# A one-core two-layer kernel: a new order from a planner that counts TensorE instructions in pieces of 256, and sums and denominators in one operation

## The chip, the core and the metric

The kernel runs on one core of one Trainium2 chip. The time is the device time of one launch in microseconds (us), the median of several runs. One further launch was taken by the profiler; the profile and the trace come from it. Engines are named as the profile names them: PE is TensorE (PEld its weight loads), DVE is VectorE, ACT is ScalarE, POOL is GpSimd, SP is SyncE, which issues most of the DMAs.

## The reference

Input `x` has 2048 rows of 512 values. Two blocks alternate, twice each, with the same weights:

```
x = x + A(layernorm(x));  x = x + B(layernorm(x))      # twice
A: q, k, v = x @ wqkv, 32 heads of 16
   phi(u) = [softmax(u @ w_phi), softmax(-u @ w_phi)]  # per head, 32 features
   kv = sum over rows of phi(k)^T v ;  z = sum over rows of phi(k)
   o  = (phi(q) @ kv) / (phi(q) . z + 1e-6) ;  return o @ wo
B: (relu(x @ W_gate) * (x @ W_up)) @ W_down            # 1376 hidden
```

The kernel does not form the softmax of the queries one by one. It keeps the exponentials (`expq`), and needs for each query and head two kinds of small numbers: the sum of the exponentials of each half (**feature sums**, made with the constant matrix `ZO`) and the product of the exponentials with `z` (parts of the **denominator**, made with `ZD`).

## The kernel before: its stages, and what sets its order

Everything stays in SBUF. The 16 tiles of 128 rows form five slabs of 2, 4, 4, 4 and 2 tiles. For each of two layers L and each slab st the stages are

- `layernorm` (L746 on): statistics on DVE, then the normalized tile (`ytile`, on ACT or DVE), then a transpose. The transpose is either a DMA (DMA_TRANSPOSE, L781), or full-size transposes on PE (L614), or, for a group of tiles, 16 transposes of 32 rows per tile (`strips`, L805).
- `keys` (L816 on): key and value products (four matmuls of 512 columns each per tile, `Wkp` and `wv`, issued by the helper `mm`, L610), exponentials of both signs on ACT (L833), their sums and reciprocals on DVE or ACT (L839 to L846), the value eviction, `vhat` on POOL or DVE (L853), and then the key-value sums: 32 matmuls per tile, each 34 columns wide (L865).
- `queries` (L913 on): query products (`Wqp`) and their exponentials (L923).
- `attend` (L926 on): 32 matmuls with `ZO` and 32 with `ZD` (both L938), an eviction of the first half (`Zs`, L951, ACT), a chain of five small operations (`zm`, `zden`, two activations, `aT`), the spreading of `aT` over the features (32 or 16 small matmuls with `EC` at L1034 for slabs 0 and 1, a round trip through DRAM for the others), the scaling of `expq`, 32 matmuls with `kvbd` (L986), four evictions (`oT`), and the product with `wo`.
- `glu`: gate and up products, ReLU (L1108), product (L1110), the down product with `Wd`, and the residual (L1056).

At the start, `load_x` and the weight loads fill SBUF (L632 to L665). `fold` (L712) multiplies the key and query weights by `w_phi` once. For the key weights it transposes 16 blocks on PE (L614), evicts them, and makes 16 matmuls against the block-diagonal matrix `BD` (L697); the query weights arrive transposed by DMA (L654).

The code only **records** operations. A list scheduler (`Program.schedule`) then places them: among the operations that are ready it takes the one that can start first, and among those the one with the lowest turn number. The turn numbers are one long list (`TURNS`, L140), one per operation. `ENG` says for single operations on which engine they run. The scheduler estimates for each operation an occupancy (`occ`) and a latency (`lat`), in ns, and `SWITCH` where PE changes between full-size and small-tile matmuls (`mode`). So an estimate changes no instruction, but it can change the order in which each engine's instructions stand. `plan` then works out the semaphore waits, and `emit` writes each engine's stream in that order; where an instruction has several waits, all but the last stand ahead of it as an instruction of their own.

The sums and the denominators are two operations unless `FUSEZ` names the slab; it is empty here:

```python
if together:
    op("pe", lambda e: (sums_q(e), dens(e))[1], reads=R_eq(st) + [R("ZO"), R("ZD"), R("ZD0")], writes=[zd], occ=2 * cost, lat=2 * cost + 200, name=f"zd{st}", mode=1)
else:
    op("pe", sums_q, reads=R_eq(st) + [R("ZO")], writes=[zd], occ=cost, lat=cost + 200, name=f"zz{st}", mode=1)
```

Of the kernel before, what the change touches and what calls it, by code (L numbers as in the profile page):

```python
# [6 lines left out]
FP32 = mybir.dt.float32  # L7
BF16 = mybir.dt.bfloat16
I32 = mybir.dt.int32
ALU = mybir.AluOpType  # L10
# [13 lines left out]
ENG = {'ap/a00/0': 'act',  # L24
 'ap/a02/3': 'dve',
 'ap/a11/0': 'act',
 'ap/a11/3': 'act',
 'ap/a12/0': 'act',
 'ap/a12/2': 'act',
 'ap/a12/3': 'act',  # L30
 'ap/a14/0': 'act',
 'ap/g00/0': 'act',
 'ap/g01/0': 'act',
 'ap/g01/2': 'act',
 'ap/g02/0': 'act',
 'ap/g03/1': 'act',
 'ap/g04/0': 'act',
 'ap/g11/1': 'act',
 'ap/g12/3': 'act',
 'ap/g13/1': 'act',  # L40
 'ap/g13/2': 'act',
# [3 lines left out]
 'em/10/00': 'act',  # L45
 'em/10/03': 'dve',
 'em/11/03': 'dve',
 'es/03/1': 'pool',
 'es/03/2': 'pool',
 'es/03/3': 'pool',  # L50
 'es/04/3': 'pool',
 'es/12/0': 'pool',
 'es/12/2': 'pool',
 'es/12/3': 'pool',
 'es/13/0': 'pool',
 'es/13/1': 'pool',
 'es/14/1': 'pool',
 'es/14/2': 'pool',
 'ot/01/2': 'dve',
 'ot/02/1': 'dve',  # L60
 'ot/02/3': 'dve',
 'ot/03/0': 'dve',
 'ot/03/1': 'dve',
 'ot/04/2': 'dve',
 'ot/11/1': 'dve',
 'ot/11/3': 'dve',
 'ot/12/1': 'dve',
 'ot/13/0': 'dve',
 'ot/13/1': 'dve',
 'ot/13/2': 'dve',  # L70
 'ot/14/2': 'dve',
 'rz/0/14': 'act',
 'rz/1/0': 'act',
 'rz/1/14': 'act',
 'rz/1/2': 'act',
 'rz/1/3': 'act',
 'rz/1/7': 'act',
 'rz/1/9': 'act',
 'vc/0/15': 'dve',
 'vc/0/5': 'dve',  # L80
 'vc/1/0': 'dve',
 'vc/1/1': 'dve',
 'vc/1/12': 'dve',
 'vc/1/13': 'dve',
 'vc/1/2': 'dve',
 'vc/1/4': 'dve',
 'vc/1/5': 'dve',
 'vh/0/1/0': 'dve',
 'vh/0/10/0': 'dve',
 'vh/0/11/1': 'dve',  # L90
 'vh/0/4/0': 'dve',
 'vh/0/5/1': 'dve',
 'vh/0/6/0': 'dve',
 'vh/1/0/0': 'dve',
 'vh/1/1/1': 'dve',
 'vh/1/11/0': 'dve',
 'vh/1/11/1': 'dve',
 'vh/1/12/0': 'dve',
 'vh/1/13/0': 'dve',
# [3 lines left out]
 'vh/1/3/1': 'dve',  # L103
 'vh/1/5/1': 'dve',
 'vh/1/7/0': 'dve',
 'vh/1/7/1': 'dve',
 'vh/1/8/1': 'dve',
 'xp/a02': 'pe',
 'xp/a14': 'sp',
 'xp/g11': 'sp',  # L110
 'yc/a02/00': 'act',
 'yc/a02/01': 'act',
 'yc/a04/1': 'dve',
 'yc/a10/02': 'dve',
 'yc/a12/00': 'dve',
 'yc/a13/00': 'dve',
 'yc/a13/02': 'dve',
 'yc/a13/03': 'act',
 'yc/a14/0': 'dve',
 'yc/a14/1': 'dve',  # L120
 'yc/g02/01': 'act',
 'yc/g02/02': 'dve',
 'yc/g03/02': 'dve',
 'yc/g03/03': 'act',
 'yc/g04/00': 'dve',
 'yc/g10/0': 'dve',
 'yc/g10/1': 'dve',
 'yc/g11/03': 'act',
 'yc/g12/02': 'dve',
 'yc/g12/03': 'act',  # L130
 'yc/g13/01': 'act',
 'yc/g13/02': 'dve'}
# [4 lines left out]
XQ = True  # L137
ZKPE = ()
FUSEZ = ()
TURNS = """  # L140
56 130 168 186 224 280 0 112 336 773 519 392 646 941 885 1404 1180 829 1068 1124 1348 1292 1236 1460 0 6 0 84 184 154 221 74 104 54 124 76 119 161 204
247 290 332 375 76 102 133 191 242 211 786 174 635 657 726 732 769 640 651 748 754 881 629 646 760 765 827 663 668 737 743 915 868 953 964 997 1199
873 942 975 992 1074 879 947 958 986 1266 885 936 970 981 1015 405 479 508 543 648 676 771 776 782 788 875 948 1134 1247 1362 1462 1526 1575 1580 1586
1631 1277 1321 1365 1409 1017 1039 1060 1082 1564 1516 1683 1849 1314 1914 2020 1743 1830 1851 1873 1959 1981 2003 2024 1929 1977 2078 2218 2211 2432
2284 2314 2529 3066 1343 1348 1354 1359 1420 1299 1304 1310 1315 1372 1387 1392 1398 1403 1468 1721 1727 1732 1738 2259 289 471 347 463 532 720 590
713 750 817 860 951 867 874 1061 992 1130 923 1223 1361 1428 1327 1395 1553 1591 1656 1699 1678 1895 1916 1938 1833 1785 1970 2390 2094 2601 2495 1504
1531 1613 1635 1483 1765 1787 1808 1689 1737 2282 2495 1881 2813 2707 2132 2154 2262 2283 2089 2111 2175 2219 2424 2472 2552 2728 2307 3328 2919 2046
2067 2240 2390 2718 2739 2761 2783 2520 2568 2770 2936 2978 3058 3216 3008 3439 3618 728 846 655 1006 1269 1559 1211 1494 1612 1679 2275 1949 1963
2355 2142 2025 2186 2561 2683 2731 2694 2660 2804 2826 2869 2891 2934 3063 3127 3214 3001 2943 3101 3279 3341 3414 3477 2847 2912 3171 3192 2955 2977
3084 3149 3389 3437 3510 3653 3602 3825 3719 3235 3257 3279 3300 3106 3343 3387 3515 3650 3485 3723 3849 3698 3931 4037 3322 3365 3408 3494 3537 3558  # L150
3623 3645 3794 3746 3891 4017 3842 4143 4249 4000 4399 4548 1567 2260 1501 2268 1625 1956 1791 2545 2616 2991 3209 3037 3051 3044 3272 3065 3134 3203
3412 3158 3285 3539 3818 3926 3947 3969 3839 3861 3882 3904 4019 4067 4140 4356 3954 4640 4421 3580 3602 3666 3688 3774 4130 4173 4216 4163 4115 4248
4398 4424 4527 4922 3710 3731 3753 3796 4054 4098 4238 4260 4211 4259 4440 4583 4472 4703 4809 4281 4453 4475 4496 4724 4745 4854 4951 4712 4664 4811
4985 5027 5197 5303 5047 5520 5597 1891 2537 2924 3049 3321 3533 3666 2878 3058 3890 3925 3999 4307 4400 4076 4152 4195 4324 4303 4346 4368 4518 4568
4616 4703 4904 4937 4760 4985 5091 4832 4897 4918 5016 4810 4973 4994 5123 5124 5172 5245 5371 5173 5542 5436 5371 5692 5747 5797 5841 5807 4648 4659
4669 4680 4691 4767 4778 4940 4979 5076 2641 2652 2663 2674 2685 2696 2707 4119 4376 4520 5219 5412 5885 5943 5977 6031 6063 6101 6167 6231 6316 6417
6291 6268 6350 6548 6691 6662 6613 6629 6746 6767 6789 6810 6832 6935 7015 6854 6875 6897 6918 6940 6993 7255 7177 7207 7245 7277 7334 7428 7433 7439
7444 7478 7184 7226 7303 7335 7416 7422 7472 7477 7526 2197 2346 2368 2498 2828 2635 4626 4875 5101 5166 5220 5316 4540 4561 4583 4702 4808 4856 2411
2433 2454 2476 2876 2780 5394 5469 5911 5990 6039 6079 6116 6159 6340 6570 6510 6451 6412 6696 6684 6749 6769 6868 6808 6817 6902 6971 7063 7111 7084
7159 7222 7450 7483 7504 7857 7157 7200 7287 7308 7368 7179 7244 7265 7330 7427 7136 7352 7373 7395 7487 7990 8068 7663 7822 7547 7814 7605 7829 8117  # L160
8152 8331 8233 8359 8240 8261 8200 8634 8380 8507 8253 7571 7579 7587 7595 8117 8169 8188 8197 8233 8338 8761 7604 7615 7713 7746 7757 7768 7778 7789
7724 7822 7877 7921 7931 7964 7986 8041 7829 8080 7888 7899 7910 7953 7975 7997 8008 8030 8325 8336 8391 8402 8413 8423 8434 8445 8069 8485 7636 7680
# [95 lines left out]
37644 37655 37666 37676 37687 37742 37760 37832 37338 37349 37414 37425 37786 37818 37829 37840 37360 37371 37393 37524 37611 37698 37731 37753 37879  # L258
37951 37447 37458 37469 37480 37491 37502 37513 37567 35994 36048 36081 36146 36254 36265 36809 37382 37607 37679 37589 37764 37796 37851 37949 37981
38036 38057 38079 38101 38122 38172 37872 37905 37927 37938 38025 38144 38155 38166 38177 38187 38209 38249 38303 37883 37894 37916 37970 38003 38014  # L260
38198 38220 38231 38242 38253 38292 38346 38253
"""

ENGINES = ("sp", "act", "pe", "dve", "pool")
# [961 lines left out]
```

## Time and profile before

| what | value |
|---|---|
| median of 3 runs | 393.76 us (393.55 to 395.07) |
| the profiled execution | 397.88 us, of it the span 396.3 us |
| granted PE clock over the span | 0.987 |
| PE busy | 382.0 us (96%), 4191 matmuls and as many weight loads |
| DVE, ACT, POOL busy | 274.3 us (69%), 196.3 us (50%), 68.5 us (17%) |
| first and last matmul | 1.55 us, 392.99 us |

The span is the time from the first to the last instruction of the profiled execution; 1.58 us lie around it. A matmul's end in the trace is modelled, so a busy PE may still be short of its best rate; the distance from one matmul's start to the next one's start is the safer number. On an undisturbed stretch this distance is 0.216 us for 512 columns and 0.109 us for 256.

### The profile page before, as it was taken

The page shows a single profiled execution, that of the slowest core. Times are in us where ns is not written, and L with a number is a line of the kernel's source. Part 1 is how long each engine was busy: PE and PEld are TensorE (multiplying, and loading weights), DVE is VectorE, ACT ScalarE, POOL GpSimd, SP SyncE. Part 2 cuts the span into 40 slices and gives each one's busy share as a digit, 9 for nine tenths or more (in the row PEclk, how much of TensorE's full clock was granted, in tenths as well). Part 3 has the DMA queues.
Part 4 walks back from the last instruction along what each step waited for, and adds up shares of the span by engine and source line. Part 5 has one row for each costly group of instructions (what it writes and reads, how often), then busy time and mean ns, then how long its engine had stood idle before and what let it go on. Part 6 is the DMA issues. An engine that isn't in the chain of part 4 may idle for free.

```text
span 396.3 us, 9884 instructions
## 1 busy us (share of the span) xinstructions
PE 382.0 (96%) x4191; PEld 203.0 (51%) x4191; DVE 274.3 (69%) x564; ACT 196.3 (50%) x427; POOL 68.5 (17%) x62
## 2 busy tenths in 40 slices
PE   5999999999999999999999979999999999999996
PEld 2544555584444544544565435558544444454564
DVE  7999967995856696775546978698684255753343
ACT  4999999860432254443425477883324121433111
POOL 0055880002500011510000523004331000000000
PEclk9799999999999999999999989999999999999999
DMA  8992200146320023010121120004552001121011
GB/s 259 324 273 56 30 3 3 45 116 120 75 60 2 12 29 80 1 17 2 40 48 23 30 31 2 4 12 129 114 145 42 13 15 41 41 54 54 2 41 46
DMA packets 51149, 24.09 MB, mean 61 GB/s; under 512 B 36801, under 2 KB 50081, under 8 KB 51105
## 3 DMA queue, kind: packets, MB, share of 16 engines
q1 hardware_dynamic: 50160, 23.11, 24.3%
q8 instruction: 33, 0.54, 0.6%
q10 hardware_dynamic: 944, 0.34, 0.3%
q14 instruction: 12, 0.09, 0.1%
HBM read 13.16 MB, written 2.42 MB: 39 GB/s over the span
## 4 chain that ended last, share of the span: by engine, by line
PE 58%; DVE 1%; issue 1%; DMA 1%; ACT 0%; SPq 0%
PE pb L610 54%; PE pb L865 1%; PE pb L938 1%; DMA yG<-ytile 1%; DVE expq L1052 1%; PE pb L986 1%; DVE x_sb L1126 0%; PE pb L1034 0%; DVE vsb L706 0%; DVE expq L1049 0%; ACT gate_sb L1108 0%; DVE hT L1110 0%; PE pb L614 0%; DVE zm L955 0%; DVE zden L957 0%
## 5 line engine op out<-in xcount | busy, mean ns | idle before, releaser
L1108 ACT ACTIVATE gate_sb<-pb 128x512 bf16<-128x512 f32 x80 | 47.1, 595 | 113.0 <-PE pb L610 95.2
L610 PE MATMUL pb<-Wd,hT 128*128 128x512 bf16 (+2 forms) x363 | 98.4, 373 | 0.0
L610 PE MATMUL pb<-yG,Wu 128*128 128x512 bf16 (+1 forms) x400 | 96.2, 336 | 0.9 <-DMA yG<-ytile 0.9
L610 PE MATMUL pb<-yG,Wg 128*128 128x512 bf16 (+1 forms) x400 | 96.2, 336 | 0.0
L1110 DVE TENSOR_TENSOR hT<-gate_sb,pb 128x512 bf16<-128x512 bf16 x80 | 53.6, 682 | 41.3 <-PE pb L610 34.2
L853 POOL TENSOR_TENSOR vhat<-vsb,rZk 128x544 bf16<-128x544 bf16 x44 | 47.4, 1101 | 151.7 <-DVE rZk L842 60.6
L1056 DVE TENSOR_TENSOR x_sb<-x_sb,pb 128x512 bf16<-128x512 bf16 x59 | 39.5, 681 | 38.3 <-PE pb L610 37.7
L610 PEld LDWEIGHTS pb<-yG,Wu 128*128 128x128 bf16 x400 | 39.0, 98 | 32.4 <-DMA yG<-ytile 1.4
L610 PEld LDWEIGHTS pb<-yG,Wg 128*128 128x128 bf16 x400 | 38.9, 98 | 30.5 <-issue 0.2
L610 PEld LDWEIGHTS pb<-Wd,hT 128*128 128x128 bf16 (+1 forms) x363 | 34.9, 98 | 34.8 <-DVE hT L1110 1.0
L839 DVE TENSOR_REDUCE Zk<-expk 128x64 f32<-128x1024 bf16 x32 | 38.3, 1204 | 7.1 <-ACT expk L833 6.8
L731 DVE BATCH_NORM_STATS2 stats<-x_sb 128x6 f32<-128x512 bf16 x60 | 40.2, 682 | 1.6 <-DMA x_sb<-in_A_x_dram 1.0
L610 PE MATMUL pb<-Wkp,yA 128*128 128x512 bf16 x128 | 40.5, 389 | 0.0
L610 PE MATMUL pb<-wv,yA 128*128 128x512 bf16 x128 | 40.1, 387 | 0.0
L833 ACT ACTIVATE expk<-pb 128x512 bf16<-128x512 f32 x64 | 35.2, 631 | 9.5 <-PE pb L610 8.2
L610 PE MATMUL pb<-wo_sb,oT 128*128 128x512 bf16 x128 | 37.7, 379 | 0.8 <-issue 0.5
L923 ACT ACTIVATE expq<-pb 128x512 bf16<-128x512 f32 x64 | 35.9, 642 | 2.9 <-PE pb L610 2.9
L610 PE MATMUL pb<-yA,Wqp 128*128 128x512 bf16 (+1 forms) x160 | 36.0, 344 | 0.4 <-ACT expk L833 0.3
L1019 POOL TENSOR_TENSOR expq<-expq,abT 128x1024 bf16<-128x1024 bf16 (+1 forms) x11 | 20.3, 1858 | 76.8 <-PE pb L610 61.8
L773 ACT ACTIVATE ytile<-x_sb,nmr,rstd 128x512 bf16<-128x512 bf16 x32 | 25.3, 829 | 5.7 <-DVE nmr L765 5.7
L1076 ACT ACTIVATE gate_sb<-pb 128x192 bf16<-128x192 f32 x16 | 5.3, 330 | 33.0 <-PE pb L610 32.5
L610 PEld LDWEIGHTS pb<-yA,Wqp 128*128 128x128 bf16 x160 | 14.8, 99 | 13.0 <-issue 1.3
(87 smaller groups left out, 341.5 us busy)
## 6 DMA issues: line engine op xcount, KB each, us to landing
abT<-spread SPq DMA_DIRECT2D x32, 128.0 KB
out_dram<-x_sb SPq DMA_DIRECT2D x15, 128.0 KB, 1.7
x_sb<-in_A_x_dram SPq DMA_DIRECT2D x3, 512.0 KB, 5.8
Wg<-in_B_W_gate_dram SPq DMA_DIRECT2D x1, 1280.0 KB, 6.8
Wu<-in_B_W_up_dram SPq DMA_DIRECT2D x1, 1280.0 KB, 11.5
Wd<-in_B_W_down_dram SPq DMA_DIRECT2D x1, 1280.0 KB, 13.3
abT<-spread SPq DMA_DIRECT2D x16, 64.0 KB
wv<-in_A_wqkv_dram SPq DMA_DIRECT2D x1, 512.0 KB
```

The source lines that it names most:

```text
L610: op("pe", lambda e: e.matmul(view(ps), lhsT, rhs, start=start, stop=stop), reads=reads, writes=[ps], occ=max(25.0, 0.4167 * n + 2.6), lat ...
L731: op("dve", lambda e: e.bn_stats(stats[:, t, :], src()), reads=[res], writes=[R("st", t)], occ=580, lat=680, name=f"bn{t}")
L773: op("act", (lambda t, yb: lambda e: e.activation(ytile[:, yb, :], x_sb[:, t, :], ACT.Identity, bias=nmr[:, t, :], scale=rstd[:, t, :]))(t ...
L833: op("act", (lambda i, s, pk: lambda e: e.activation(expk[:, i, s, :], full(pk), ACT.Exp, scale=1.0 - 2.0 * s))(i, s, pk), reads=[pk], wri ...
L839: op("dve", (lambda i, zb: lambda e: e.tensor_reduce(Zk[:, zb, :], expk[:, i, :, :].rearrange("p s (h f) -> p (s h) f", f=16), AX.X, ALU.a ...
L853: op(eng, (lambda i, s, vb, rz: lambda e: e.tensor_tensor(vhat[:, i, s, :, :], vsb[:, vb, :, :], rZk[:, rz, s * 32:(s + 1) * 32].unsqueeze ...
L923: op("act", (lambda c0, s, ps: lambda e: e.activation(eqv(st)[:, c0:c0 + per, s, :], ps.f32()[:, 0:per * n].rearrange("p (c n) -> p c n", ...
L1019: op(eng, lambda e: e.tensor_tensor(part, part, abT[:, c].rearrange("p (s n) -> p s n", s=2)[:, :, 0:n], ALU.mult), reads=Re + [R("abT", c ...
L1056: op("dve", lambda e: e.tensor_tensor(x_sb[:, t, :], x_sb[:, t, :], full(ps), ALU.add), reads=[R("x", t), ps], writes=[R("x", t)], occ=597 ...
L1076: op("act", (lambda gate, ps, half: lambda e: e.activation(gate, half(ps, 0), ACT.Relu))(gate, ps, half), reads=[ps], writes=[R("gate", gb ...
L1108: op("act", (lambda gb, pg, k: lambda e: e.activation(gate_sb[:, gb, 0:k], pg.f32()[:, 0:k], ACT.Relu))(gb, pg, k), reads=[pg], writes=[R( ...
L1110: op("dve", (lambda gb, hb, pu, k: lambda e: e.tensor_tensor(hT[:, hb, 0:k], gate_sb[:, gb, 0:k], pu.f32()[:, 0:k], ALU.mult))(gb, hb, pu, k),
```

## The change

All of the change is in the planner, in how it is fed, and in three places of the recorded work.

1. The scheduler counts PE's instructions, two for each matmul. At instruction 193, and every 256 after it, it puts a boundary, and keeps two boundaries at least 3.7 us apart (9 us in the first 25 us). Semaphore waits are not counted.
2. Estimates are changed: key-value sums, sums and denominators, the products at the former L986, and SP's DMA issue.
3. All turn numbers are new, and some 145 entries of `ENG` are added, taken out or changed.
4. `FUSEZ` names seven of the ten pairs of layer and slab: slabs 2 to 4 of the first layer and 1 to 4 of the second. There the 32 matmuls with `ZO` and the 32 with `ZD` follow each other as one operation.
5. The key weights come in four DMAs of 128 KB in place of two of 256 KB; `fold` transposes and evicts them by the row block that one DMA brings, in place of the column block that needs all four. `wv` is loaded through ACT's queue in place of SP's.
6. Layernorm "a10" transposes by DMA in place of `strips`.

A third way to make the sums (`ZALL`, with a DRAM tensor) is added in the code, but its list is empty, so it records nothing.

```diff
-FUSEZ = ()
+FUSEZ = ((0, 2), (0, 3), (0, 4), (1, 1), (1, 2), (1, 3), (1, 4))
+ZALL = ()
 TURNS = """
...
-    DMA_ISSUE = {"sp": 560.0, "act": 560.0, "pool": 1100.0}
+    DMA_ISSUE = {"sp": 600.0, "act": 560.0, "pool": 1100.0}
...
+    CHUNK, CHUNK0 = 256, 193
+    FETCH, FETCH0 = 3700.0, 9000.0
...
             if o.eng == "pe":
                 mode = o.mode
+                while chunk < count + 2 * o.ins:
+                    part = (chunk - count) / (2 * o.ins)
+                    at = s + o.occ * part
+                    came = crossed + (self.FETCH if at > 25000.0 else self.FETCH0) if chunk > self.CHUNK0 else 0.0
+                    if at < came:
+                        if chunk == count:
+                            s += came - at
+                        else:
+                            o.occ, o.lat = o.occ + came - at, o.lat + came - at
+                        at = came
+                    crossed = at
+                    chunk += self.CHUNK
+                count += 2 * o.ins
+            o.start = s
...
-        def load_wk(eng, c):
-            dma(eng, lambda e: e.dma_start(Wknat[:, c:c + 2, :], wqkv_v[:, c:c + 2, 512:1024]), writes=R_Wnat["k"][c:c + 2], nbytes=262144, name="ld wk")
+        def load_w(w, c, eng):
...
+                dma(ENG.get(f"ld/w{w}{c}", eng), lambda e: e.dma_start(Wnat[:, c:c + 1, :], wqkv_v[:, c:c + 1, o:o + 512]), writes=[R_Wnat[w][c]], nbytes=131072, name=f"ld w{w}{c}")
...
         def fold(w, Wnat, Wout):
-            for kc in range(0 if XQ and w == "q" else 4):
-                ps = bank(f"wt{w}{kc}")
-                for ic in range(4):
+            for ic in range(4):
+                if ic in XW[w]:
+                    continue
+                ps = bank(f"wt{w}{ic}")
+                for kc in range(4):
...
-                   writes=[ps], occ=225 * len(js), lat=200 + 225 * len(js), name=f"kv{st}", mode=1)
+                   writes=[ps], occ=286 * len(js) - 72, lat=128 + 286 * len(js), name=f"kv{st}", mode=1, ins=32 * len(js))
...
-            cost = 32 * max(8.0, w / 9.6)
+            cost = 41 + 3.33 * w
...
-               writes=pns, occ=80 + n, lat=280 + n, name=f"num{st}", mode=3)
+               writes=pns, occ=62 + 0.835 * n, lat=262 + 0.835 * n, name=f"num{st}", mode=3, ins=32)
```

## The prediction

> **What bounds the kernel now.** I read the page first, then the chain of waits, then PE's rows in order of time.
>
> ```profile
> PE 382.0 (96%) x4191; PEld 203.0 (51%) x4191; DVE 274.3 (69%) x564; ACT 196.3 (50%) x427; POOL 68.5 (17%) x62
> ...
> q8 instruction: 33, 0.54, 0.6%
> ```
>
> PE has work all the time, and no other engine comes near it. So time can only go where PE stands still or runs slowly. The second line is easily passed over: a queue that moves instructions, 33 transfers. PE's records in the trace are 4191 matmuls, 4191 weight loads and 80 of its sequencer (78 semaphore waits, 2 drains), 8462 in all, and 8462 / 33 = 256. PE's program is fetched in pieces of 256.
>
> ```profile
> 229.34 1.30 PE pb L865 x124
> 230.65 2.01 issue
> 232.66 0.20 PE pb L865 x4
> ```
>
> This is the chain of waits. "issue" means that PE waited for nothing the profile shows, in the middle of one operation. PE's own rows show four more such stops (their lengths in brackets in the rows): 0.32 us before 65.43, 0.49 before 172.84, 0.64 before 252.46 and 0.45 before 267.12. Counting all PE records, waits too, the five instructions at which PE goes on are numbers 2241, 4289, 5313, 6081 and 6849, each 193 plus a multiple of 256, to the instruction. From the passing of the boundary before to the resumption it is 3.76, 3.62, 4.5, 3.68 and 3.60 us. So PE stops where it uses up 256 instructions in less than some 3.65 us. A 512-column matmul pair takes 0.216 us, so 128 of them last 28 us and hide a fetch; small matmuls do not:
>
> ```profile
> 61.48 0.87 PE L938 MATMUL pb<-expq,ZD 128*32 128x64 bf16 x64
> 62.17 0.63 PE L938 MATMUL pb<-expq,ZO 128*32 128x128 bf16 x32
> 62.73 1.70 PE L610 MATMUL pb<-yA,Wqp 128*128 128x256 bf16 x11
> ```
>
> Start to start, 64 pairs (128 instructions) pass in 0.69 us. The five stops cost, start to start and less the usual distance, 0.55 + 0.62 + 2.34 + 0.87 + 0.61 = 5.0 us.
>
> ```profile
> 235.60 1.06 PE L610 MATMUL pb<-Wkp,yA 128*128 128x512 bf16 x2
> ...
> 239.45 0.81 PE L610 MATMUL pb<-Wkp,yA 128*128 128x512 bf16 x3
> ```
>
> After the longest stop, from 233.89 to 237.29, eight 512-column matmuls stand 0.427 us apart, not 0.216: the granted clock was halved for 3.4 us. Price 8 x 0.21 = 1.7 us. All other waits of PE after 28 us add up to some 2.1 us (1.04 at 92.6 for a transpose DMA, 0.38 at 157.1, the rest under 0.3 each).
>
> ```profile
> 7.69 0.62 PE L614 MATMUL pb<-ident,hT 128*128 128x128 bf16 x8 [2.02 <-DMA hT<-in_A_wqkv_dram]
> ...
> 12.30 1.91 PE L610 MATMUL pb<-wv,yA 128*128 128x512 bf16 x4
> ```
>
> At the start PE waits for the second half of the key weights until 7.69, then for `BD` until 10.28, and dense work begins at 12.30, at half clock until 15.4.
>
> **The change, part by part.** The profiled execution took 397.88 us, its span 396.3; the median of the plain runs is 393.76, that is 4.1 less. I work out differences and put them on the median; what the plain runs lack of the stops above cannot be seen.
>
> *Small-tile changes of PE.* Counted over both instruction orders, PE changes between full-size and small-tile forms 87 times before and 73 times after: seven fused pairs, and the layernorm that no longer uses strips. A change costs some 0.1 us: 32 `ZO` matmuls with full-size work behind them take 0.56 us (62.17 to 62.73), and in the rows where another small group of the same form follows 0.447. 14 x 0.1 = 1.4 us, plus the 32 strip transposes, 0.2: **-1.6 us**. Both ends: 14 x 0.08 (entering a small group) and 14 x 0.115 (leaving one), -1.3 to -1.8. What fusing delays (`Zs` can only be evicted after both halves, and sums can't be taken before the key-value sums are there) lies 0.45 us earlier in a chain through ACT and DVE that other matmuls cover; uncovered it costs 0.45 us in each of seven slabs, 3.2 at worst, which I keep for the range.
>
> *The pieces.* The planner now holds boundaries 3.7 us apart, but it counts two for each matmul and no waits. The trace counts the waits, so the real boundaries come earlier in the order than the planner's, by some 30 instructions at 65 us and 80 at the end. I added up the rows' distances over the new order, between real boundaries (193 + 256k, waits counted). By the planner's own count no piece is under 3.6 us. By the real count four are:
> - 1985 to 2241: the end of a 64-column `ZD` group, three 128-column groups (3 x 0.447), two changes, three 512-column matmuls (0.65), 26 of `EC` (0.2): 2.4 us, 1.25 short.
> - 4545 to 4801: four and one of 256 columns, three of 512, 119 of L865 (1.0): 2.3 us, 1.35 short.
> - 5569 to 5825: 60 of L865, five of 512, 32 of L865, 31 of `ZO`: 2.2 us, 1.45 short.
> - 6337 to 6593: 11 of `ZO`, three groups of 0.447, 20 of the 512-column `kvbd`: 1.9 us, 1.75 short.
>
> The same sum over the order of before gives 0.43, 0.72, 1.65, 0.93 and 0.69, near the five stops, and a sixth, 1.09 before 5825, that did not come: the boundary ahead of it lay in dense 512-column work, and there the fetch began 1.5 us before PE reached it. The 4545 boundary lies in 256-column work, so its stop may be hidden too. New stops 4.5 to 5.8 against 5.0: **+0.2 us**, from -0.6 (and less, where a data wait fills the same gap) to +1.0.
>
> [...]
>
> *The clock.* Only a stop of over 2 us halved it in the row of before; the new ones are at most 1.75. In the profiled execution that is -1.7 us, in the plain runs, which may not have had it, 0. I take **-0.5**.
>
> *The start.* SP's queue has 1024 KB of `x` ahead of the two key-weight DMAs in place of 896, and `wv` (512 KB) now moves beside them from ACT's queue. At 324 GB/s (second slice of the page) that is 0.4 us later, up to 2.0 with equal shares: last landing 8.1 to 9.7 in place of 7.69. But `BD` now stands in DVE's order right behind the first statistics, so that from the landing it is transposes 0.4, eviction 0.75, products 0.4 to 0.8: dense work begins at 9.7 to 11.7 in place of 12.30. Until 15.4 the clock is half, so half of the gain stays: **-0.5 us**, from -1.3 to +1.0 (the three evictions of `Wkp` stand in a row on ACT).
>
> *All else.* New turn numbers move every instruction by a little. Counts by engine hardly change (ACT loses six half-size `oT` evictions to DVE, six reciprocals go from DVE to ACT as two activations of 0.27 us each); DVE stays near 69%. SP issues two layernorm transposes more. The 2.1 us of data waits can become 1 to 5; I take them as unchanged.
>
> Sum: -1.6 + 0.2 - 0.5 - 0.5 = -2.4 us, so 393.76 - 2.4 = **391.4 us**; in a profiled execution some 395.5.
>
> **Rivals.**
> *Stops gone.* If PE's real boundaries are where the planner puts them (no waits counted), all stops go: -1.6 - 5.0 - 0.5 - 0.5 = -7.6, 386.2 us. Against it: with waits left out, the sum over the order of before gives no stop at 232.66 and a false one of 2.2 us.
> *Clock, slower.* The four stops of 1.25 to 1.75 us each halve the clock for the next 3.4 us; each then costs 1.7 more. All four: -1.6 + 1.0 - 0.5 + 6.8 = +5.7, 399.5; three (-1.6 + 0.2 - 0.5 + 5.1 = +3.2) 397.0; two 395.3. It decides from the third such halving on. For it: the halving came after 2.2 us idle, a part of its 3.4 us. Against it: stops of 0.6 to 0.9 did nothing. [...]
> *New data waits.* The two or three us saved come back as waits (a late DRAM round trip of `aT`, a late transpose, the fused sums' 0.45 us a slab): +1.5 to +5 on 391.4, 393 to 396.5.
>
> **How the numbers follow.** 0.5% of 393.76 is 2.0 us, about what a measurement of this kernel tells from no change; faster means under 391.8, slower over 395.7. Forecast 0.62 (own range 389 to 394; 0.38 of it faster, 0.24 within 0.5%), stops gone 0.08 (faster), data waits 0.18 (0.13 within, 0.05 slower), clock 0.12 (slower). That is 0.46, 0.37 and 0.17. The range 387.0 to 396.5 takes in the forecast and the data waits and leaves out most of the other two.
>
> **What would show it.** In the changed profile: "issue" stops of PE at records 193 + 256k, the longest ahead of 6593, 5825 and 2241, and none over 2 us; some 73 changes; no halved clock after the first 16 us; `wv` matmuls before 12 us. The forecast is wrong if PE shows stops at other places, no stops, or more than 4 us of waits for ACT, DVE or DMAs after 28 us.

## The result, and the profile after

The changed kernel takes 396.32 us (median of 18 runs, 394.64 to 398.63) against 394.17 us for the kernel before (median of 18, 393.06 to 396.42). The ratio is 1.0048, with a 95% interval of 1.0028 to 1.0069: slower by some 2 us, where 2.4 us less was forecast. A second set of runs side by side gave 1.0026 (0.9992 to 1.006). The loss is small, but the sign of the forecast was wrong.

The page of the changed kernel, in the two lines that answer to those of before (busy time of each engine; the instruction queue):

```profile
PE 373.6 (95%) x4107; PEld 203.3 (52%) x4159; DVE 274.2 (69%) x561; ACT 195.8 (50%) x431; POOL 71.2 (18%) x63
...
q8 instruction: 32, 0.52, 0.6%
```

PE is busy for 8 us less than in the profile of before (382.0), in a span that is only 1.6 us shorter (394.7 against 396.3). A part of that is not real: this trace holds 4107 matmuls for 4159 weight loads, so 52 records of matmuls are missing, where the trace of before has all of its 4191. Up to the last matmul PE is idle for 17.6 us, of which 2.7 lie at missing records; before it was 11.0. So it stands still some 4 us more. Its rows in order of time show where (start, length, form, count; in brackets the idle time before the row and what ended it):

```profile
62.96 0.38 PE L1143 MATMUL pb<-aT,EC 32*128 32x64 bf16 x26
64.73 0.23 PE L1143 MATMUL pb<-aT,EC 32*128 32x64 bf16 x6 [1.39 <-issue]
...
68.19 0.40 PE L1143 MATMUL pb<-aT,EC 32*128 32x128 bf16 x16 [0.58 <-DVE expq L1161]
...
70.52 0.23 PE L1022 MATMUL pb<-expq,ZD 128*32 128x128 bf16 x4
71.36 0.57 PE L1022 MATMUL pb<-expq,ZD 128*32 128x128 bf16 x28 [0.61 <-issue]
...
244.69 0.45 PE L1022 MATMUL pb<-expq,ZO 128*32 128x64 bf16 x31
246.21 0.19 PE L1022 MATMUL pb<-expq,ZO 128*32 128x64 bf16 x1 [1.06 <-issue]
...
259.19 0.61 PE L1095 MATMUL pb<-expq,kvbd 32*32 32x512 bf16 x20
260.74 0.43 PE L1095 MATMUL pb<-expq,kvbd 32*32 32x512 bf16 x12 [0.94 <-issue]
```

Read the counts first: 26 and 6, 4 and 28, 31 and 1, 20 and 12. Each pair is one operation cut in two with no wait named, at instructions 2241, 2497, 5825 and 6593, all 193 plus a multiple of 256. Three of them are those that the prediction named as the longest. From start to start, less the usual distance, they cost some 5.2 us together, inside the 4.5 to 5.8 forecast. The 0.58 us before 68.19 is of another kind: PE waits for DVE.

To see where an execution loses time I add up the rows' usual distances over the instruction order (372.94 us before, 371.48 after, so the new order is 1.46 us shorter) and look at how far PE is behind that sum. This is what each stretch adds, in us, for the profiled executions. The stretches are counted in the sum of rows, which runs some 10 us behind the clock of the trace:

| execution | its time | first 50 us | 50 to 75 | 75 to 220 | 220 to 255 | behind 255 |
|---|---|---|---|---|---|---|
| before (that of the prediction) | 397.88 | 10.40 | 1.33 | 6.00 | 1.96 | -0.12 |
| before, `b_same` | 391.98 | 10.07 | 1.33 | 1.48 | 0.84 | -0.07 |
| before, `b_again` | 396.72 | 10.12 | 1.32 | 5.64 | 1.47 | -0.13 |
| after | 396.52 | 9.63 | 3.61 | 2.42 | 3.67 | -0.14 |
| after, `a_again` | 394.53 | 8.76 | 3.64 | 1.57 | 3.36 | -0.15 |

Two things stand out. The new order loses 2.3 us more in the attention of the first layer (50 to 75) and about 2 us more in that of the second (220 to 255), alike in both executions. And the old order loses some 6 us between 75 and 220 in two executions of three, and 1.5 in the third.

### The profile page after: what moved, and what is told of

It reads as the page before. It is cut to its first block, busy times and chain, and to the rows that moved or that the text cites. A ratio compares the mean times of both kernels' runs of the same rounds, so it can differ in the third digit from the quotient of the medians.

```text
span 394.7 us, 9764 instructions
## 1 busy us (share of the span) xinstructions
PE 373.6 (95%) x4107; PEld 203.3 (52%) x4159; DVE 274.2 (69%) x561; ACT 195.8 (50%) x431; POOL 71.2 (18%) x63
## 3 DMA queue, kind: packets, MB, share of 16 engines
HBM read 13.16 MB, written 2.42 MB: 39 GB/s over the span
## 4 chain that ended last, share of the span: by engine, by line
PE 73%; ACT 12%; DVE 6%; DMA 5%; issue 2%; SPq 1%; DVEq 0%
PE pb L679 68%; ACT expk L906 4%; ACT expq L1007 3%; DMA hT<-in_A_wqkv_dram 2%; PE pb L1022 2%; ACT ytile L846 2%; PE pb L938 1%; DMA yG<-ytile 1%; DVE expq L1161 1%; PE pb L1095 1%; DMA abT<-spread 1%; ACT vsb L780 1%; DVE Zk L912 1%; ACT gate_sb L1217 1%; DMA yA<-ytile 1%
## 5 line engine op out<-in xcount | busy, mean ns | idle before, releaser
L679 PE MATMUL pb<-Wd,hT 128*128 128x512 bf16 (+3 forms) x353 | 93.8, 372 | 0.7 <-issue 0.5
L679 PE MATMUL pb<-yG,Wu 128*128 128x512 bf16 (+1 forms) x394 | 92.9, 336 | 1.0 <-DMA yG<-ytile 0.3
L679 PE MATMUL pb<-yG,Wg 128*128 128x512 bf16 (+1 forms) x394 | 91.7, 336 | 0.4 <-issue 0.2
L679 PE MATMUL pb<-wv,yA 128*128 128x512 bf16 x119 | 37.3, 379 | 1.3 <-DMA yA<-ytile 0.5
L679 PE MATMUL pb<-Wkp,yA 128*128 128x512 bf16 x122 | 37.9, 379 | 0.6 <-issue 0.3
L1128 POOL TENSOR_TENSOR expq<-expq,abT 128x1024 bf16<-128x1024 bf16 (+1 forms) x13 | 23.6, 1824 | 79.6 <-PE pb L679 53.2
L679 PE MATMUL pb<-wo_sb,oT 128*128 128x512 bf16 x123 | 34.9, 379 | 0.7 <-issue 0.3
L679 PE MATMUL pb<-yA,Wqp 128*128 128x512 bf16 (+1 forms) x150 | 32.3, 334 | 1.8 <-issue 1.0
## 6 DMA issues: line engine op xcount, KB each, us to landing
Wd<-in_B_W_down_dram SPq DMA_DIRECT2D x1, 1280.0 KB, 15.4
```

What stands on the lines that cost most here:

```text
L679: op("pe", lambda e: e.matmul(view(ps), lhsT, rhs, start=start, stop=stop), reads=reads, writes=[ps], occ=max(25.0, 0.4167 * n + 2.6), lat ...
L1128: op(eng, lambda e: e.tensor_tensor(part, part, abT[:, c].rearrange("p (s n) -> p s n", s=2)[:, :, 0:n], ALU.mult), reads=Re + [R("abT", c ...
```

## The experiments

My theory was that the place of the 256-instruction boundaries among the small tiles decides, and that the forecast had compared with an unusual execution. The rival was that the new order (its fused operations, or the rest of it) makes new waits for data.

### The same kernels again

No edit. `b_same` and `b_again` are the kernel before, `a_again` is the changed one.

> The kernel before again, unchanged, for a second profile of it with its granted clock. Theory 1 (the profiled execution of before that the prediction was built on was a slow one, by its halved clock and by some more): span near 392.5 us, device time 394 +-1, the five stops at the same instructions (2241, 4289, 5313, 6081, 6849), no halved clock in the middle in most runs. Rival (the halved clock behind the 2.2 us stop belongs to every run): span near 396 again, with eight 512-column matmuls 0.43 us apart behind 232.7.

> The kernel before a third time, for its stops: 5.0 us and a halved clock in the execution that the prediction read (397.88 us), 1.3 us and none in b_same's (391.98). If 5.0 was the usual amount: stops of 4 to 5.5 us behind 28 us, a halved clock behind 16 us, a profiled time near 397. If it was an outlier and the stops differ from execution to execution: 1 to 3.5 us, 392 to 395.

> The changed kernel a second time. If its stops are as little fixed as those of before: 2 to 6 us, at other boundaries than 2241, 5825 and 6593. If they are fixed by the order (the boundaries lie among small tiles that follow waits, where the sequencer cannot be ahead): stops at these three again, 4 to 5.5 us, 395.5 to 397.

`b_same`: 394.27 us, ratio to before 0.9989 (0.996 to 1.0019). `b_again`: 394.38, ratio 0.9989 (0.9956 to 1.0022). `a_again`: 395.86, ratio 1.0026 (0.9992 to 1.006).

PE's rows at the key-value sums, first in `b_again`, then in `b_same`:

```profile
228.88 1.38 PE L865 MATMUL pb<-vhat,expk 128*32 128x34 bf16 x124
232.00 0.20 PE L865 MATMUL pb<-vhat,expk 128*32 128x34 bf16 x4 [1.74 <-issue]
...
233.78 1.06 PE L610 MATMUL pb<-Wkp,yA 128*128 128x512 bf16 x2
```

```profile
228.26 1.43 PE L865 MATMUL pb<-vhat,expk 128*32 128x34 bf16 x128
...
232.01 0.81 PE L610 MATMUL pb<-yA,Wqp 128*128 128x512 bf16 x3
```

It is the same program. In `b_again` the operation is cut at 124 and 4 and stands for 1.74 us, and the 512-column matmuls behind it are 0.43 us apart (two take 1.06, and 0.59 at the full clock): the stop and the halved clock that the prediction had read. In `b_same` all 128 run in one row, and three 512-column matmuls take 0.81, the full rate. What differs is the transfer of the instruction queue (q8) that belongs to the boundary before, 5057 (193 + 19 x 256): it began 2.9 us before PE came to that boundary in `b_same`, and 1.6 to 1.7 us after it in the two others. All stops of before behind 28 us, start to start and less the usual distance, are 5.0, 1.3 and 4.1 us in the three executions; those of after are 5.2 and 5.0, at the same four boundaries both times. So the stops of the old order come and go, and those of the new one stood at the same places in both of its traces. The execution that the forecast was read from had the most of them, and was 3.7 us above its own median. But `b_again` is near it, as the first half of its expectation said, so a long stop at 5313 is no rarity. The plain runs say more: the six sets of runs of before beside these experiments hold 143 executions with a median of 394.2 us. Only 5 took longer than 397.88, and only 1 less than the 391.98 of `b_same`. The traces of before lie near the two ends.

### Moving the boundaries

Tiny matmuls at the end of the warm-up, where PE waits for the input anyway (3.09 us ahead of 8.21 in the changed kernel's trace), move every later boundary to an earlier place in an unchanged order:

```diff
+        def warm_up(e, i):
+            ins = e.matmul(full(warm), ones[:, 0:128], ones[:, 0:512], start=True, stop=True)
+            for k in range(SHIFT if i == NWARM - 1 else 0):
+                q = 32 * (k % 4)
+                ins = e.matmul(warm.f32()[q:q + 32, 0:34], ones[:, 0:32], ones[:, 0:34], start=True, stop=True, skip_group_check=True, tile_position=(0, q))
+            return ins
```

> The changed kernel; the last warm-up operation issues 102 more tiny matmuls (34 columns) whose results nobody reads, so that all piece boundaries lie 204 instructions earlier in the same order. Theory of the pieces (a stop where 256 PE instructions, waits counted, pass in under 3.65 us): the sum of the short pieces falls from 5.8 (measured stops 4.4) to 2.3 us, almost all of it near the L0 attention; the time falls by 2 to 3.4 us against the changed kernel, to about 393.5, if the extra matmuls lie in PE's wait for the first transposed tile (3.1 us). Rival (stops come from waiting data or from where the planner put its boundaries): no change, or up to 2 us slower for the extra matmuls.

> The changed kernel with 40 more tiny matmuls at the end of the warm-up (results unread): boundaries 80 instructions earlier, the worst place found for this order. Theory of the pieces: short pieces sum to 9.3 in place of 5.8 us, stops ahead of records 1985 (1.6), 5313 (1.9), 5825 (1.0), 6081 (0.7) and 6593 (1.9), so +2 to +3.5 us against the changed kernel, about 399. Rival (data waits set the end): no change within 1 us.

> The kernel before with 50 more tiny matmuls at the end of the warm-up (results unread): boundaries 100 instructions earlier. Theory of the pieces: short pieces fall from 5.5 to 2.1 us, the stops ahead of 4289, 5313 and 6849 are gone, so -2 to -3.4 us against the kernel before, about 391.5. Rival: no change.

> Before with 124 tiny matmuls at the end of its warm-up, the boundaries 248 instructions earlier, at nearly the worst place for this order: short pieces 6.3 us by the program (2.1 in b_shift50, 5.5 in before), of it 3.2 between 62 and 220 and 2.7 behind 220. If the order of before suffers from the boundaries as that of after does (a_shift40 against a_shift102: 7.9 us measured for 7.0 by the program): 396.5 to 398. If the old order is proof against them, since its small tiles stand apart and the sequencer runs ahead: 393 to 394.5.

| kernel | median us | ratio to before (95%) | short pieces by the rows |
|---|---|---|---|
| `a_shift102` | 394.35 | 0.9986 (0.9954 to 1.0018) | 2.3 |
| `a_shift40` | 402.25 | 1.0194 (1.0152 to 1.0236) | 9.3 |
| `b_shift50` | 393.09 | 0.9961 (0.9933 to 0.999) | 2.1 |
| `b_shift124` | 395.6 | 1.0033 (1.0002 to 1.0065) | 6.3 |

With nothing else changed, the place of the boundaries moves the new order by 0.0208, that is 8 us, and the old one by 0.0072, 2.8 us. PE's rows of `a_shift40`:

```profile
28.41 0.62 PE L947 MATMUL pb<-vhat,expk 128*32 128x34 bf16 x59
32.75 0.22 PE L947 MATMUL pb<-vhat,expk 128*32 128x34 bf16 x5 [3.72 <-issue]
...
35.44 1.06 PE L679 MATMUL pb<-Wkp,yA 128*128 128x512 bf16 x2
```

One stop of 3.72 us, at a time when the weights' DMAs still run in the changed kernel's trace (165 GB/s from 28 to 32 us, 5 from 32 to 36), and half clock behind it (512-column matmuls 0.42 to 0.43 us apart). This one place makes 6 of the 9.3 us between the profiled executions of `a_shift40` (403.89) and `a_shift102` (394.59), and the expectation had no stop there. Set against the changed kernel itself (1.0048 and 1.0026), `a_shift102` (0.9986) is 1.6 to 2.4 us faster: moving the boundaries alone takes back what the changed kernel had lost (its interval lies clear of the first set's, and overlaps that of the second). So the boundaries are shown to matter. `b_shift50`, the old order with 50 tiny matmuls, has the lowest ratio of this study, and its interval lies below 1. The sizes were not well foretold: `a_shift102` and `b_shift50` came out 0.9 and 1.6 us above their expectations, `a_shift40` 3 us above, and `b_shift124` between its two.

But the pair `a_shift102` and `b_shift50` also speaks for the rival. Their short pieces are the same (2.3 and 2.1), and the new order, 1.46 us shorter by its rows, is still 0.0025, 1.0 us, slower, though the two intervals overlap. By these numbers some 2.4 us go to something else.

### The stop by itself

`b_tail` puts 1536 independent small matmuls of three widths behind the last instruction of PE:

```diff
+            for width, times in ((34, 512), (64, 512), (128, 512)):
+                for k in range(times):
+                    q = 32 * (k % 4)
+                    ins = e.matmul(tail.f32()[q:q + 32, 0:width], ones[:, 0:32], ones[:, 0:width], start=True, stop=True, skip_group_check=True, tile_position=(0, q))
```

> Before with a ladder of 1536 independent small matmuls on TensorE behind its last one (its outputs go unused): 512 of 34 columns, 512 of 64, 512 of 128, all 32x32 tiles on four row quarters' columns in turn. It measures the disputed cost by itself: 256 instructions are 128 matmuls, by the rows 2.1, 3.5 and 7.1 us. If a piece that passes in under 3.65 us makes TensorE stop: 3.65 us for each piece of the first two widths, 7.1 for the third, 57 us in all, 450 to 453. If the instructions come in time whatever the pace: 8.4 + 14 + 28 = 51 us, 444 to 446, and no gaps in the ladder.

432.24 us in one execution, 38 us more than before, where 51 or 57 were expected: both expectations were wrong on the work, because these matmuls, on four column groups in turn, pass faster than I had worked out (128 of 34 columns in 1.2 us, not 2.1). The rows settle the question all the same:

```profile
388.04 2.02 PE L1176 MATMUL pb<-yG 128*32 128x34 bf16 x218
392.21 1.19 PE L1176 MATMUL pb<-yG 128*32 128x34 bf16 x128 [2.16 <-issue]
395.66 1.23 PE L1176 MATMUL pb<-yG 128*32 128x34 bf16 x128 [2.26 <-issue]
399.39 1.70 PE L1176 MATMUL pb<-yG 128*32 128x34 bf16 x128 [2.50 <-issue]
```

128 matmuls with their weight loads are 256 instructions. They run in 1.2 us (1.7 in the last row, at half clock), then PE stands for 2.2 to 2.5 us with nothing to wait for. From 392.21 on, ten pieces take 3.70 us in the mean from start to start (3.45 to 4.0), at all three widths. So this ladder shows the cost of a boundary bare, among small tiles. Among large ones it doesn't show: in the trace of before the last 313 matmuls, of 192 to 512 columns, make 626 instructions with their weight loads and hold three boundaries (343.4, 367.9 and 387.5 us); they run for 54.06 us without a stop, no two starts over 0.22 us apart:

```profile
338.50 54.06 PE pb L610 x313
```

### Fusing in the planner's hands

`a_unfused102` and `a_unfused12` are the changed kernel with `FUSEZ` empty and seven turns added; `b_fused58` and `b_fused82` the kernel before with the `FUSEZ` of after and seven turns left out. The numbers are those of the tiny matmuls. The cut is from the second pair; the first has it the other way round.

```diff
-FUSEZ = ()
+FUSEZ = ((0, 2), (0, 3), (0, 4), (1, 1), (1, 2), (1, 3), (1, 4))
```

> The turn numbers, engines and loads of after with nothing fused (seven turns added for the denominators, one product behind the sums), and 102 tiny matmuls: short pieces 2.3 us, as in a_shift102, its partner, which took 394.35, and at the same places (all among the small tiles of the first layer's attention). Changes of tile size rise from 73 to 84, the sum of rows by 1.1. Theory: 395.4 (394.6 to 396.2). Rival 'fusing itself costs': 394.3 or less.

> As a_unfused102 with 12 tiny matmuls: short pieces 1.6 us, of which 0.1 among the first layer's small tiles (2.3 in a_unfused102) and 1.4 among those of the second. If a stop costs its length wherever it falls: 0.7 less than a_unfused102, 394.7 by the theory. If a stop in the first layer's attention costs more than its length there, since DVE and ACT run out of work behind it and PE then waits for them in turn, up to twice: 392.5 to 393.8.

> The order of before with the seven fused operations alone (the turns of the seven denominator operations are left out), and 58 tiny matmuls more at the end of the warm-up, so that the boundaries lie where the pieces that are too short sum to 2.2 us by the program (2.1 in b_shift50, its partner, which took 393.09). Changes of tile size fall from 87 to 80. Theory 'a change of tile costs its 0.19 us, and the pieces their shortness': 393.1 - 0.7 = 392.4 (391.6 to 393.2). Rival 'fusing itself costs': the feature sums come out one product later, and ACT and DVE, which wait for them, start later: 393.6 or more.

> As b_fused58, with 82 tiny matmuls: short pieces 1.7 us by the program, 0.4 to 0.5 of them among the small tiles of the first layer's attention (1.05 in b_fused58). Theory: 391.9 (391.0 to 392.8), the fastest so far. Rival 'fusing itself costs': 393.2 or more.

| kernel | median us | ratio to before (95%) |
|---|---|---|
| `a_unfused102` | 394.57 | 0.9993 (0.9966 to 1.002) |
| `a_unfused12` | 396.0 | 1.0049 (1.002 to 1.0079) |
| `b_fused58` | 394.54 | 0.9999 (0.9974 to 1.0024) |
| `b_fused82` | 396.52 | 1.0043 (1.0019 to 1.0068) |

Taking the fused operations out of the new order adds 1.1 us to the sum of rows and 0.3 us to the time, within the intervals. Putting them into the old one takes 0.7 off the sum and adds 1.5 us against `b_shift50`, with intervals that overlap too. By these numbers the saved changes of tile size are given back. `a_unfused12` and `b_fused82` missed their forecasts by 1.3 and 4.6 us, and the sum of short pieces alone doesn't explain them. In their traces PE waits for data, which the sum leaves out: 1.4 us near 159 for a layernorm transpose and 0.8 near 258 for ACT in `b_fused82`, 1.0 near 282 for a transpose in `a_unfused12`. These kernels also don't part cause from cause: the planner, with other estimates, moved other matmuls as well (in `b_fused58` eight query matmuls that had stood between the numerators and the spread now stand ahead of the numerators).

### Fusing with nothing else moved

To part them, the order of before was written out for every engine and kept, with 50 tiny matmuls as in `b_shift50`, and only the denominators' 32 products of six slabs were put right behind the sums:

```diff
+        for line in ORDER.values():
+            line = [self.ops[int(k)] for k in line.split()]
+            for a, b in zip(line, line[1:]):
+                b.odeps.add(a.idx)
```

`b_fix50` does that. `b_two50` gives the denominators a PSUM bank of their own, so that ACT may copy the sums while PE goes on. `b_bank50` is `b_fix50` with every bank where before has it. `b_port50` also keeps which DVE operation each GpSimd multiply waits for. `b_first50` is `b_port50` with only the first layer's slabs fused. (With no slab fused this last form should be the program of `b_shift50`; that was not run.) `a_two102` does to the new order what `b_two50` does to the old one.

> The order of before on every engine written out and kept, with six fused operations (slabs 2 to 4 of both layers) where the sums stood, and the 50 tiny matmuls of b_shift50, its partner (393.09): so nothing moves but the denominators' 32 products. Sum of rows 0.5 less than b_shift50's, short pieces 0.6 more (2.8 to 2.1). Theory 'changes of tile and short pieces are all': 393.2 (392.6 to 393.8). Rival 'the sums come late': ACT copies them only when the fused operation has ended, 0.2 to 0.6 us later for each slab, and the chain behind (DVE, ACT, spread matmuls) is late by it six times: 394 to 395.

> As b_fix50, instruction for instruction on TensorE, but sums and denominators are two operations with a PSUM bank each, so ACT may copy the sums while TensorE makes the denominators. Theory: as b_fix50. Rival 'the sums come late': it gives back what b_fix50 lost, 392.6 to 393.3.

> The order of after on every engine written out and kept, with 102 tiny matmuls as in a_shift102, its partner (394.35), but sums and denominators of the seven fused slabs as two operations with a PSUM bank each, so the sums may be copied 0.2 to 0.6 us earlier; short pieces as in the partner (2.3). If the late sums are what the new order loses to the old one: 393.0 to 393.8. If not: 394.3 (393.9 to 394.8).

> b_fix50 again, but with every PSUM bank where before has it: b_fix50 had kept the order and let the planner choose the banks anew, and TensorE then waited for banks that ScalarE's evictions released late (1.7 us between 262 and 290 us alone). Now the instructions of TensorE, VectorE and ScalarE stand as in b_shift50 (393.09), its partner, except that the denominators' 32 products of six slabs stand right behind the sums. Sum of rows 0.5 less, short pieces 0.6 more (2.8 to 2.1). If banks were what b_fix50 lost, and fusing itself costs nothing: 393.2 (392.6 to 393.8). If the late sums cost: 394 to 395, with waits for DVE and ACT at the spread matmuls behind each fused slab.

> b_bank50 again (398.69), but GpSimd's multiplies wait for the same VectorE operations as in before. In b_bank50 the planner, whose times had moved, let two of them go ahead of VectorE's, and the trace shows VectorE's aT product taking 1.96 us for 0.41 and its expq product 2.61 for 0.69, each while a GpSimd multiply of 2.1 us ran: 3.5 us in all. Now order, banks and this order of the two engines are those of b_shift50 (393.09), and only the denominators' products of six slabs have moved. If those two meetings were the loss: 395.2 (394.6 to 395.8). If fusing by itself costs nothing beyond rows and short pieces: 393.2. If the loss is elsewhere: 398 or more.

> As b_port50, with only the three slabs of the first layer fused. Sum of rows 0.2 less than b_shift50's (393.09), short pieces 0.6 more, of them 0.6 where the first fused operation now stands (53 us of the rows). If fusing costs through short pieces alone: 393.5. If the sums' late copy costs as well, 0.4 us or so at the spread matmuls (TensorE waited 0.9 us for ScalarE there in b_bank50): 393.9 to 394.4. The difference to b_port50 is what the second layer's three slabs cost.

| kernel | median us | ratio to before (95%) | against its partner |
|---|---|---|---|
| `b_fix50` | 398.56 | 1.0134 (1.0105 to 1.0162) | +6.8 us |
| `b_two50` | 397.98 | 1.0112 (1.0081 to 1.0143) | +6.0 us |
| `b_bank50` | 398.69 | 1.01 (1.0054 to 1.0146) | +5.5 us |
| `b_port50` | 395.43 | 1.0024 (1.0005 to 1.0044) | +2.5 us |
| `b_first50` | 394.4 | 0.9987 (0.9959 to 1.0015) | +1.0 us |
| `a_two102` | 394.79 | 1.0003 (0.9978 to 1.0029) | +0.7 us |

The last column is the difference of the ratios times 394 us, the partner being `b_shift50` or, in the last row, `a_shift102`.

The banks were not it: `b_bank50` loses as much as `b_fix50`, against my theory of the moment. What the first three share is seen on DVE, here in `b_bank50` (start, length), and on POOL:

```profile
268.36 1.96 DVE L1110 TENSOR_TENSOR aT<-Zs,zr 128x256 bf16<-128x256 f32 x1
...
273.71 2.61 DVE L1169 TENSOR_TENSOR expq<-expq,abT 128x1024 bf16<-128x1024 bf16 x1
```

```profile
267.91 2.13 POOL L1169 TENSOR_TENSOR expq<-expq,abT 128x1024 bf16<-128x1024 bf16 x1 [24.10 <-PE pb L751]
271.52 4.26 POOL L1169 TENSOR_TENSOR expq<-expq,abT 128x1024 bf16<-128x1024 bf16 x2 [1.48 <-DVE x_sb L1206]
```

The same two operations take 0.41 and 0.68 us in `b_shift50`. In `b_fix50` they take 1.88 and 2.61, in `b_two50` 1.68 and 2.60. In `b_bank50` each ends 0.3 to 0.5 us after a GpSimd multiply that began before it: 1.55 + 1.93 = 3.5 us more on DVE. With the fused operations' times the planner had let POOL go first. `b_port50` puts this back and is 3.3 us faster than `b_bank50` by the medians, 3.0 by the ratios, near the 395.2 that was expected. In both products the loss is near what was left of the GpSimd multiply when the product began: 1.68 us for the first and, with the two multiplies of the second row taken as equally long, 2.07 for the second.

What `b_port50` still loses is 2.5 us, where the rows promised a gain of 0.5 and the short pieces a loss of 0.6. Not all that its trace shows is the price of fusing. That execution was the slowest of its twelve (397.14), and has this ahead of the first fused operation:

```profile
30.13 0.25 PE L964 MATMUL pb<-ident,ytile 32*128 32x32 bf16 x13 [1.75 <-issue]
...
31.09 1.84 PE L760 MATMUL pb<-wv,yA 128*128 128x512 bf16 x4
```

It is a stop of 1.75 us with half clock behind it, where `b_shift50` stops for 1.03 us at the same instruction and goes on at full clock; 1.9 us of the distance between the two traces arise here. `b_first50`, the same up to this point, has 1.16 us and full clock. How many of the plain executions have the long stop is open. The rest of the distance arises at the fused operations of the first layer. PE's rows there, in `b_port50` and then in `b_shift50`:

```profile
66.09 0.29 PE L1097 MATMUL pb<-expq,ZD 128*32 128x128 bf16 x8
67.22 0.52 PE L1097 MATMUL pb<-expq,ZD 128*32 128x128 bf16 x24 [0.84 <-issue]
...
69.30 0.41 PE L1193 MATMUL pb<-aT,EC 32*128 32x64 bf16 x32
69.65 0.39 PE L760 MATMUL pb<-yA,Wqp 128*128 128x512 bf16 x1
70.91 0.41 PE L1193 MATMUL pb<-aT,EC 32*128 32x128 bf16 x16 [0.87 <-ACT abT L868]
```

```profile
65.92 0.41 PE L1043 MATMUL pb<-aT,EC 32*128 32x64 bf16 x32
66.26 0.63 PE L947 MATMUL pb<-expq,ZD 128*32 128x128 bf16 x32
66.83 0.39 PE L610 MATMUL pb<-yA,Wqp 128*128 128x512 bf16 x1
67.53 0.40 PE L1043 MATMUL pb<-aT,EC 32*128 32x128 bf16 x16 [0.31 <-ACT abT L718]
```

This is the mechanism. From one spread (`EC`) to the next it is 1.61 us in both kernels (69.30 to 70.91, 65.92 to 67.53), because PE has to wait until ACT has copied the first one out. In the old order the denominators' `ZD` products stand in that gap and fill 0.57 us of it, and 0.31 us of waiting is left. Fused, they are gone from the gap, and the wait is 0.87 us, 0.56 more. The time that they took there was never on the path; where they stand now, it is. And standing behind the sums they make 64 matmuls, 128 instructions, in a row, and a boundary that falls there stops PE for 0.84 us ahead of the query matmuls that ACT waits for. Between 50 and 75 us of the sum of rows `b_port50` and `b_first50` both lose 3.27 us to `b_shift50`'s 1.33, 1.94 more.

The late copy of the sums, my own rival, is there and costs nothing here. ACT's rows in `b_port50`:

```profile
67.79 0.38 ACT L1110 ACTIVATE Zs<-pb 128x256 f32<-128x256 f32 x1 [0.41 <-PE pb L1097]
69.19 1.08 ACT L1082 ACTIVATE expq<-pb 128x512 bf16<-128x512 f32 x2 [1.02 <-PE pb L760]
70.16 1.10 ACT L868 ACTIVATE abT<-pb 128x512 bf16<-128x512 f32 x2
```

The copy (`Zs`) waits 0.41 us for the fused operation, and behind it ACT waits another 1.02 us for the query matmuls. `b_two50` and `a_two102`, where ACT may copy the sums early, gain nothing beyond the intervals either, and `b_first50`, though its time lies in the range that I had given to the late copy, has the same two waits (0.45 and 1.02 us). In the second layer the picture is less clear: behind 84 us `b_port50` falls 0.3 us further behind `b_shift50`, and `b_first50`, which is not fused there, makes up 0.5. These are single traces, and how the loss of the second layer comes about stays open.

## Why the prediction was wrong, point by point

*Small-tile changes of PE, -1.6.* The rows agree: the new order is 1.46 us shorter. The time doesn't follow. The step that failed here is to count row time that is saved as time that is saved, with no more against it than that the sums come late in a chain "that other matmuls cover". The denominators' products were themselves such a cover: out of the gap between two spreads they leave 0.56 us more of waiting. The late sums, to which the sentence gave a price of up to 3.2 us, were covered where the trace was read. In the old order six fused slabs cost 2.5 us by the ratios, 1.94 of it seen at the first layer's, in place of gaining 0.5; in the new order seven gain 0.3 of 1.1, within the intervals.

*The pieces, +0.2.* "New stops 4.5 to 5.8 against 5.0": the first half held, in both executions (5.2, 5.0), at three of the places named; the one before 4801 was nearly hidden (the 128 matmuls around it stand in one row of 1.35 us, from 212.19 on), as was thought possible, and one came at 2497 that was not named. There the fetch began 6.0 us after the boundary before it, behind PE's wait for DVE at 68.19. The second half failed, and it is the largest of the failed steps: 5.0 was the largest of three values, 5.0, 1.3 and 4.1. With their mean of 3.5, against 5.1 of after, the term is +1.6, with the lowest +3.8. The prediction saw that its execution was 4.1 us above the median and that the plain runs' stops "cannot be seen", and then took them as 5.0 all the same.

*The clock, -0.5.* Two of three executions of before had the halved clock behind the stop at 5313, worth 1.7 us each; none of after had it there. The mean is -1.1.

*The start, -0.5.* Dense work begins at 13.19 us (12.31 in `a_again`), later than the 9.7 to 11.7 forecast and not ahead of 12 us as the signs demanded. But its matmuls stand at full-clock distance from the second one on (13.7 us; 12.8 in `a_again`), where the halved clock lasted until 15.4 in the execution that was read and until 14.6 in the two others of before:

```profile
10.01 0.61 PE L683 MATMUL pb<-ident,hT 128*128 128x128 bf16 x4 [0.21 <-DMA hT<-in_A_wqkv_dram]
...
13.19 1.08 PE L679 MATMUL pb<-wv,yA 128*128 128x512 bf16 x3
```

At 50 us the two executions of after are 9.63 and 8.76 behind their rows, those of before 10.40, 10.07 and 10.12: -1.0. The sign was foreseen, but for another reason: the forecast had the dense work begin earlier, and it is the clock that rose earlier. That is luck, and the size is not firm: the mean clock of the changed kernel's plain executions goes from 0.990 to 1.000.

*All else, unchanged.* This failed. Behind 50 us, with stops and halved clock taken off, 2.5, 2.3 and 2.5 us are left in the executions of before and 4.3 and 3.4 in those of after: +1.4. This is for the greater part PE's waiting for data: the waits of over 0.2 us that name an engine or a DMA add up to 1.1, 0.9 and 1.9 us before and 2.6 and 1.7 after, 0.9 of the 1.4. That is the rival "new data waits", if a little under the +1.5 to +5 that it was given.

*Sum.* By the means -1.5 + 1.6 - 1.1 - 1.0 + 1.4 = -0.6; against `b_same`, which had neither long stop nor halved clock there, -1.5 + 3.8 - 1.0 + 1.4 = +2.7. The medians of the plain runs say +2.15 and +1.0, between the two. Which share of the plain runs of before has the long stop at 5313 cannot be seen without a trace, and stays open. Their mean clock, which is on record, gives a hint: it was 0.987 in both traced executions that had the halved clock at the start and at 5313, and 10 of the 143 plain ones lie that low, with 396.6 to 399.0 us. Executions with a shorter halving at the start can hide the one at 5313.

*The rivals.* "Stops gone" did not happen: instructions 193 + 256k count the waits, as read. "Clock, slower" did not happen in the changed kernel (its stops are under 1.7 us), but `a_shift40` shows that it can, behind a stop of 3.72 us. "New data waits" was right in kind, and had too little weight (0.18).

## What to carry to other kernels

Read a term that is compared from more than one execution, above all one that the plain median disagrees with: a stop that depends on when the fetch began (2.9 us ahead of a boundary or 1.6 behind it) comes and goes in one and the same program. Before small work is packed closer, ask what gap it fills where it stands (0.57 us of `ZD` products here, with 0.56 us more of waiting once they were gone), for its rows' time is saved only if nothing waits there. Here small tiles pass 256 instructions in less than the 3.70 us that a piece took (1.2 us for 128 matmuls of 34 columns in `b_tail`), and the place of the boundary was worth more than the better order: 8 us between two places in the new order, against 1.46 us of rows. Moving it cost 50 or 102 tiny matmuls in an idle warm-up.

## What the runs showed of the hardware that was not expected

- A run of small tiles alone, with no wait, goes at 3.70 us for each 256 instructions in the mean of ten (`b_tail`), and PE stands for up to two thirds of it.
- In that ladder the granted clock was halved for 23.9 us (from 394.0), with no stop longer than 2.5 us, and came back while stops of 1.8 to 2.0 us went on. Two windows of it (busy time and count of PE, PEld, DVE, ACT, POOL, then the clock, the DMA share and GB/s):

```profile
396.00:400.00 4.00, 1.50 (x171) 1.40 (x162) 0.00 (x0) 0.00 (x0) 0.00 (x0) 0.50 0.02 4
...
420.00:424.00 4.00, 1.97 (x128) 1.82 (x128) 0.00 (x0) 0.00 (x0) 0.00 (x0) 1.00 0.02 4
```

- Two DVE products took 1.96 and 2.61 us for 0.41 and 0.68 beside GpSimd multiplies of 2.1 us (`b_bank50`); the first multiply began 0.45 us ahead of its DVE product there, and 0.54 us behind it in `b_shift50`, where nothing was lost.
